# Chunked attention and a gated feed-forward layer on one core: late exp written contiguously, queries kept in mod-3 order, no block-diagonal query tile, and the first two blocks in a fixed list of steps

## The chip, the cores and the metric

The kernel runs on one core of a Trainium2 chip. The metric is the device time in microseconds. Before the change, three runs took 261.99, 262.46 and 265.42 us; the median is 262.46 us. The profile is of one more execution.

## The reference

Chunked attention with memory (B = 4, H = 8, S = 768, D = 64, chunks of 32 queries that see 16 keys to the left, 8 to the right and 8 memory keys), and then a gated feed-forward layer on the 3072 tokens.

```python
for c in range(S // 32):
    lo, hi = max(0, 32 * c - 16), min(S, 32 * c + 40)
    k_full = concat(mem_k, k[:, :, lo:hi]); v_full = concat(mem_v, v[:, :, lo:hi])
    scores = (q[:, :, 32 * c:32 * c + 32] @ k_full.T) / 8
    a = softmax(scores)
    attn[:, :, 32 * c:32 * c + 32] = a @ v_full
x = attn as [3072 tokens, 512]
out = (maximum(x @ w_gate, 0) * (x @ w_val)) @ w_out      # 512 -> 1536 -> 512
```

## The kernel before

The 3072 tokens are cut into eight **blocks** of 384 tokens (half a batch entry). The attention of a block is four **steps** of 96 queries against a band of 120 keys and 8 memory keys. A step is: the scores matmuls, exp on ScalarE, a multiplication with a 0/1 mask on VectorE, eight values matmuls (`L261`, one per head, which also give the row sums), a reciprocal and a normalising product on VectorE (`L270`), and a transposition into `xT`. The feed-forward part of a block is twelve **units** (`dff`, `L286`), each with four gate matmuls (`L293`), a relu on ScalarE (`L296`), four value matmuls (`L298`) and the product of the two on VectorE (`L300`), into `gvT`. After them come three **output tiles** (`outp`, `L306`) of twelve matmuls each (`L309`), copied to `o_sb` by ScalarE and stored.

The steps of blocks 3 to 7 stand inside the units of the block ahead (loop at `L557`): scores and exp ahead of units 4, 6, 8 and 10, the mask behind that unit's product, the values ahead of the unit two further on. The engines run their own instructions in order, as the code issues them; `mask` is issued after `dff`, so it stands behind that unit's product on VectorE. Units use four PSUM banks in turn (`bank()`, `NG`), so a gate matmul of one unit needs the relu or the product of two units earlier to be done.

Keys and queries are loaded as float32 with three consecutive tokens on a partition (`load3`), so that the token number modulo 3 becomes an axis `t`. After the cast they are turned, by TensorE in blocks 0 and 1 (called early), by DMA transposes on SyncE's queue in the others (`turn_k`, `turn_q`, `turn_dma`). `bands` copies the keys into the bands `kb`. In the late blocks `diag` (`L186`) copies the turned queries of two heads into a block-diagonal tile `qd`, so that one matmul of 192 columns over 128 rows gives the scores of two heads (`L237`). The queries there have the order (t, c), and the late exp (`L250`) puts them back in token order as it writes: every third element of a 16-bit row. The early scores (`L233`) are eight matmuls of 96 columns over 64 rows, with queries in token order, and the early exp (`L246`) writes runs.

Blocks 0 and 1 go through `pipe` (`L439`), ten rounds of one step each, with the casts, turns and weight loads of block 1 between them; values are gathered by selection matmuls (`gather_v`), with a leading one (`L347`) for the memory rows. The last four rounds hold one unit of block 0 each. Filler matmuls on zeros (`keep`) stand between the first rounds. Then come the other 20 units of blocks 0 and 1, and then their six output tiles, with the four steps of block 2 between them. The weights are loaded on GpSimd's queue: columns 0 to 255, 256 to 511, 512 to 1023 and 1024 to 1535 of both matrices and three pieces of `w_out`, all in a row; a one-element write into `kraw` after the last piece of `w_val` holds back the loads of block 2's keys and queries.

## Time and profile before

| | before |
|---|---|
| median of three runs | 262.46 us |
| the profiled execution | 262.1 us |
| its span, first to last instruction | 260.4 us |
| TensorE busy | 235.4 us, 90% |
| VectorE, ScalarE, GpSimd busy | 124.1, 128.4, 49.3 us |
| mean granted clock of TensorE | 0.985 of full speed |
| loads of a block's keys and of its queries | 768 KB each |
| loads of a 512-column piece of w_gate or w_val, of a piece of w_out | 512 KB each as stored |

A row of the timeline has the start in us, the duration in us, the engine, the line of the kernel, what is written and read with its shape, and how many instructions are merged in the row; in brackets stands how long the engine was idle ahead of it and what released it. The durations of matmuls are modelled and reach past the start of the next, so distances between starts are the better measure. PE is TensorE, DVE is VectorE, ACT is ScalarE, POOL is GpSimd, and SPq is the queue of DMAs that SyncE issues.

### The profile page before, as it was taken

How to read it: one execution, taken by the hardware profiler on the slowest of the kernel's cores; microseconds unless marked ns; L12 is line 12 of the kernel's file. 1: busy time of each engine (PE TensorE's matmuls, PEld its weight loads, DVE VectorE, ACT ScalarE, POOL GpSimd, SP SyncE). 2: the span in 40 equal slices, each digit the busy share in tenths (PEclk: the TensorE clock that was granted, in tenths of full speed). 3: DMA queues.
4: the chain of work that ended last, by engine and by line, in shares of the span. 5: the costliest groups of instructions: out<-in, count | busy, mean ns of one | idle time of the engine just before them, and what ended most of it. 6: DMA issues, size and time to landing. Idle time of an engine off the chain costs nothing.

```text
span 260.4 us, 4350 instructions
## 1 busy us (share of the span) xinstructions
PE 235.4 (90%) x1611; PEld 131.5 (50%) x1611; DVE 124.1 (48%) x257; ACT 128.4 (49%) x197; POOL 49.3 (19%) x96
## 2 busy tenths in 40 slices
PE   8895899999989698898989989898899998999993
PEld 3353565666444355544554555445564555446641
DVE  3776573444654057604673076605753276504410
ACT  2564554365357256643673457443772555333321
POOL 6499920000000500006000420006000500000000
PEclk9998899999999899999999999999999999999999
DMA  6999999849973997159941997179912801121012
GB/s 209 312 270 138 183 207 247 219 94 177 294 193 115 202 285 131 30 124 259 237 96 32 241 281 146 33 168 276 234 39 71 198 0 33 30 86 39 0 40 82
DMA packets 84381, 39.37 MB, mean 151 GB/s; under 512 B 57096, under 2 KB 81416, under 8 KB 84360
## 3 DMA queue, kind: packets, MB, share of 16 engines
q1 hardware_dynamic: 78408, 34.25, 54.2%
q0 software_dynamic: 5808, 4.72, 12.1%
q8 instruction: 12, 0.20, 0.3%
q10 hardware_dynamic: 144, 0.13, 0.1%
q14 instruction: 9, 0.07, 0.1%
HBM read 30.05 MB, written 6.29 MB: 140 GB/s over the span
## 4 chain that ended last, share of the span: by engine, by line
PE 56%; DVE 16%; issue 8%; DMA 7%; ACT 6%; SPq 3%; POOL 0%; ACTq 0%; DVEq 0%; POOLq 0%
PE PS L309 19%; PE PS L298 14%; PE PS L293 13%; DVE gvT L300 5%; DVE ex L257 5%; PE PS L261 4%; ACT g_relu L296 4%; DMA qT<-qn 3%; DVE x_big L270 3%; DMA vraw<-in_mem_v_dram 2%; PE PS L352 2%; DMA vx<-in_v_dram 2%; PE PS L237 2%; SPq L141 2%; DVE qd L188 1%
## 5 line engine op out<-in xcount | busy, mean ns | idle before, releaser
L300 DVE TENSOR_TENSOR gvT<-PS,g_relu 128x384 f16<-128x384 f32 x96 | 53.0, 556 | 96.3 <-PE PS L298 75.0
L293 PE MATMUL PS<-xT,w_gate_sb 128*128 128x384 f16 x384 | 78.7, 328 | 2.7 <-issue 2.2
L298 PE MATMUL PS<-xT,w_val_sb 128*128 128x384 f16 x384 | 79.1, 329 | 2.1 <-DVE gvT L300 1.9
L296 ACT ACTIVATE g_relu<-PS 128x384 f16<-128x384 f32 x96 | 47.8, 498 | 43.4 <-PE PS L293 22.4
L309 PE MATMUL PS<-w_out_sb,gvT 128*128 128x512 f16 x288 | 64.1, 379 | 0.0
L298 PEld LDWEIGHTS <-w_val_sb 128*128 128x128 f16 x384 | 37.8, 99 | 28.1 <-issue 3.8
L293 PEld LDWEIGHTS <-w_gate_sb 128*128 128x128 f16 x384 | 37.2, 98 | 25.9 <-issue 4.3
L250 ACT ACTIVATE ex<-PS 128x768 f16<-128x768 f32 x24 | 35.2, 1468 | 20.3 <-PE PS L237 20.2
L309 PEld LDWEIGHTS <-gvT 128*128 128x128 f16 x288 | 27.7, 98 | 31.4
L319 ACT COPY o_sb<-PS 128x512 f32<-128x512 f32 x23 | 13.5, 587 | 44.9 <-PE PS L309 43.0
L204 POOL COPY kb<-kT 128x320 f16<-128x320 f16 (+1 forms) x15 | 11.0, 830 | 130.2 <-DMA kT<-kn 130.2
L261 PE MATMUL PS<-vb,ex 128*128 128x66 f16 x256 | 13.6, 195 | 9.9 <-DVE ex L257 8.7
L270 DVE TENSOR_TENSOR x_big<-PS,rinv 96x512 f16<-96x512 f32 x32 | 22.0, 686 | 1.1
L261 PEld LDWEIGHTS <-ex 128*128 128x128 f16 x256 | 11.1, 99 | 20.4 <-ACT g_relu L296 15.6
L257 DVE TENSOR_TENSOR ex<-ex,mask_int 128x768 f16<-128x768 f16 x24 | 14.1, 586 | 7.3 <-ACT ex L246 3.9
L237 PE MATMUL PS<-qd,kb 128*128 128x192 f16 x96 | 11.8, 245 | 0.1
L188 DVE COPY qd<-qT 64x1536 f16<-64x1536 f16 x12 | 8.4, 696 | 4.8 <-DMA qT<-qn 4.8
L165 ACT CAST qn<-qraw 128x768 f16<-128x768 f32 x12 | 10.0, 836 | 0.0
L267 DVE RECIPROCAL rinv<-PS 96x8 f32<-96x8 f32 x32 | 6.4, 201 | 7.5 <-PE PS L261 5.4
L165 ACT CAST kn<-kraw 128x768 f16<-128x768 f32 x12 | 9.9, 827 | 0.0
L376 PE MATMUL PS<-zero 128*128 128x512 f16 x20 | 7.7, 519 | 1.3 <-DVE zero L378 1.3
L352 PE MATMUL PS<-v,step 128*120 128x512 f16 x27 | 8.8, 450 | 0.0
(90 smaller groups left out, 122.7 us busy)
## 6 DMA issues: line engine op xcount, KB each, us to landing
out_dram<-o_sb SPq DMA_DIRECT2D x23, 256.0 KB
vraw<-in_v_dram SPq DMA_DIRECT2D x24, 240.0 KB
kraw<-in_k_dram SPq DMA_DIRECT2D x7, 768.0 KB
qraw<-in_q_dram SPq DMA_DIRECT2D x7, 768.0 KB
w_out_sb<-in_moe_w_out_dram POOLq DMA_DIRECT2D x3, 512.0 KB, 18.1
w_gate_sb<-in_moe_w_gate_dram POOLq DMA_DIRECT2D x2, 512.0 KB, 10.4
w_val_sb<-in_moe_w_val_dram POOLq DMA_DIRECT2D x2, 512.0 KB, 12.0
kraw<-in_k_dram SPq DMA_DIRECT2D x2, 384.0 KB
```

The source lines that it names most:

```text
L165: eng(d.rearrange("p a t (x d) -> p a x t d", x=2), raw[c][:, i, 2 * a0:2 * a0 + 2 * na].rearrange("p (a x) t d -> p a x t d", x=2))
L237: pe.matmul(o[:, :, 0:QB].rearrange("p x (t c) -> p x t c", t=R3), lhsT=self.kb[:, a, j, :], rhs=qd_t[i][:, a].rearrange("p x (t c) -> p x ...
L250: act.activation(e.rearrange("p h (c t) -> p h t c", t=R3), s_ps.rearrange("p h (t c) -> p h t c", t=R3), ACT.Exp, scale=SCALE)
L257: dve.tensor_tensor(out=e, in0=e, in1=m8, op=ALU.mult)
L261: pe.matmul(PS[:, 2 + h // 4, VW * (h % 4):VW * (h % 4) + VW], lhsT=self.ex[:, h, :], rhs=self.vb[:, self.j, h, :], start=True, stop=True)
L270: dve.tensor_tensor(out=self.x.rearrange("p (b h d) -> p b h d", b=2, h=4), in0=o[:, :, :, 0:D], in1=rb, op=ALU.mult)
L293: pe.matmul(g_ps, lhsT=w_gate_sb[:, f, 128 * m:128 * m + 128], rhs=xTs[n][:, f, c0:c1], start=(f == 0), stop=(f == NFC - 1))
L296: act.activation(g_relu[:, 0:w], g_ps, ACT.Relu)
L298: pe.matmul(vl_ps, lhsT=w_val_sb[:, f, 128 * m:128 * m + 128], rhs=xTs[n][:, f, c0:c1], start=(f == 0), stop=(f == NFC - 1))
L300: dve.tensor_tensor(out=gvT[n][:, m, c0:c1], in0=vl_ps, in1=g_relu[:, 0:w], op=ALU.mult)
L309: pe.matmul(PS[:, o], lhsT=gvT[n][:, m, 128 * t:128 * t + 128], rhs=w_out_sb[:, m, :], start=(m == 0), stop=(m == NDC - 1))
L352: pe.matmul(o[0:BAND], lhsT=step3[:, c:c + BAND], rhs=v16[:, w, :, t, :], start=False, stop=(e == len(mm) - 1), skip_group_check=True)
```

## The change

What it does, part by part:

- **Late scores.** `qd` and `diag` are gone. Each late step has eight matmuls of 96 columns over 64 rows, which read the turned queries as they lie, in the order (t, c).
- **Late exp.** All exps have the early form and write runs; the queries stay in the order (t, c) through mask, values, normalisation and `xT`. The masks of the late blocks are built in that order.
- **Product.** For blocks 2 to 7 the product writes `gvT` in the order (t, j, c) and reads both its operands so, in runs of 32. An output tile then holds every third token, and its rows are stored 3 rows apart.
- **Blocks 0 and 1.** `pipe` is replaced by `ORDER`, a list of 190 tokens; each token issues one operation. It holds the eight steps and eight units (0 to 3 of each block). Scores have two pairs of banks in turn, `ex` four buffers. In steps 0, 2 and 3 the mask is added to the scores by matmuls with the identity (`pm`), in the other five VectorE multiplies. The keys' bands of block 0 are gathered by selection matmuls (`keys`); the memory rows of the values come by DMA (`vm16`) and not by a leading selection matmul. Filler matmuls stand only at the start.
- **Behind the list.** The 16 units left hold block 2's four steps (ahead of units 7, 9, 11, 13, values two units later), and all six output tiles stand at the end. The loads of block 2's keys and queries are held back by the piece of `w_gate` with columns 512 to 1023, and the last weight pieces are loaded after that; `w_out` is loaded behind block 2's bands and a first load of its values.

```diff
         def scores(self):
             i, j = self.n % 2, self.j
+            if self.pm:
+                m = neg[self.kd]
+                m4 = bass.AP(tensor=m.tensor, offset=m.offset, ap=[m.ap[0], [0, HP], [1, QB]])
+                for x in range(2):
+                    pe.matmul(PS[:, self.sb + x, 0:HP * QB].rearrange("p (a c) -> p a c", a=HP), lhsT=id16, rhs=m4,
+                              start=True, stop=True)
             for a in range(HP):
-                if self.early:
-                    for x in range(2):
-                        pe.matmul(PS[:, x, QB * a:QB * a + QB], lhsT=self.kb[D * x:D * x + D, a, j, :],
-                                  rhs=qp[D * x:D * x + D, i, a, QB * j:QB * j + QB], start=True, stop=True)
-                else:
-                    o = PS[:, a // 2, 256 * (a % 2):256 * (a % 2) + 256].rearrange("p (x c) -> p x c", x=2)
-                    pe.matmul(o[:, :, 0:QB].rearrange("p x (t c) -> p x t c", t=R3), lhsT=self.kb[:, a, j, :],
-                              rhs=qd_t[i][:, a].rearrange("p x (t c) -> p x t c", t=R3)[:, :, :, PP * j:PP * j + PP],
-                              start=True, stop=True)
+                for x in range(2):
+                    r = slice(D * x, D * x + D)
+                    o = PS[:, self.sb + x, QB * a:QB * a + QB]
+                    if self.early:
+                        pe.matmul(o, lhsT=self.kb[r, a, j, :], rhs=qp[r, i, a, QB * j:QB * j + QB],
+                                  start=not self.pm, stop=True, skip_group_check=self.pm)
+                    else:
+                        pe.matmul(o.rearrange("p (t c) -> p t c", t=R3), lhsT=self.kb[r, a, j, :],
+                                  rhs=qT_t[i][r, a, :, PP * j:PP * j + PP], start=True, stop=True)
...
-                s_ps = PS[:, 0:2].rearrange("p b (h c) -> p (b h) c", h=4)[:, :, 0:QB]
-                act.activation(e.rearrange("p h (c t) -> p h t c", t=R3),
-                               s_ps.rearrange("p h (t c) -> p h t c", t=R3), ACT.Exp, scale=SCALE)
+            act.activation(self.ex[:, :, 0:QB].rearrange("p (h b) c -> p b h c", b=2),
+                           PS[:, self.sb:self.sb + 2, 0:HP * QB].rearrange("p b (h c) -> p b h c", h=HP), ACT.Exp, scale=SCALE)
...
+        if n in EARLY:
+            dve.tensor_tensor(out=gvT[n][:, m], in0=vl_ps, in1=g_relu, op=ALU.mult)
+        else:
+            dve.tensor_tensor(out=gvT[n][:, m].rearrange("p (t j c) -> p t j c", t=R3, j=NJ),
+                              in0=vl_ps.rearrange("p (j t c) -> p t j c", t=R3, j=NJ),
+                              in1=g_relu.rearrange("p (j t c) -> p t j c", t=R3, j=NJ), op=ALU.mult)
...
+        if n in EARLY:
+            dst = out[n * MB + 128 * t:n * MB + 128 * t + 128, :]
+        else:
+            dst = bass.AP(tensor=out.tensor, offset=out[n * MB + t, 0].offset,
+                          ap=[[R3 * DM, 128], [1, DM]])
...
+    keep(20)
...
+        b3:P x6:A P4 S7 x7:A M5:D g7:A n4:D G6 fg00 P5 g6:A T4 e4:A fv00 M6:D
+        n5:D fg03 M7:D P6 fr00:A n6:D fg02 T5 fg01 fr03:A fm00:D e5:A fr02:A P7 n7:D T6 fv03 fv01 e6:A T7 fm03:D
...
+    pl(raw["k"][0:1, 0, 0, 0, 0:1], w_gate_sb[0:1, 0, 1023:1024])
     load_kq(2)
+    load_w(1024, 512)
+    cast_kx(pl, 1)
+    units = [(n, m) for m0 in (4, 8) for n in (0, 1) for m in range(m0, m0 + 4)]
+    cast3(ac, "k", 2, 0, 2)
+    cast3(ac, "k", 2, 2, 2)
+    turn_k(2)
+    cast3(ac, "q", 2, 0, 2)
+    cast3(ac, "q", 2, 2, 2)
+    turn_q(2)
+    hook = {
+        0: [lambda: load_v(2, 0), lambda: load_v(2, 1), lambda: load_v(2, 2), lambda: load_v(2, 3)],
+        1: [lambda: bands(2, pl)],
+        2: [lambda: pl(gate, vraw[0:1, 0, 1, 0, 0:1]), lambda: load_wo(0), lambda: load_wo(4), lambda: load_wo(8)],
+        6: [lambda: cast_v(dv, 2, 0, 2)],
+        7: [lambda: cast_v(dv, 2, 2, 2)],
+        12: [lambda: load_kq(3)],
+        13: [lambda: load_v(3, 0), lambda: load_v(3, 1), lambda: load_v(3, 2), lambda: load_v(3, 3)],
+    }
+    su, vu = (7, 9, 11, 13), (9, 11, 13, 15)
...
                 if u == 0:
-                    diag(n + 1)
-                if u == 1:
                     bands(n + 1, pl)
```

In the two lines of `ORDER` shown, S is a step's scores, x its exp, M its mask, P its values, n its normalisation, T and e the turn into `xT`, G and g a gather of values and its copy, fg, fr, fv and fm the four parts of a unit; the letter behind the colon is the engine.

ScalarE, from the last copies into `xT` of the early blocks to block 2. Before, the casts of block 2's keys (`kn`) and queries (`qn`) stand late among the 20 units:

```order
L280 COPY xT<-PS 128x4x96
L296 ACTIVATE g_relu<-PS 128x384 x12
L165 CAST kn<-kraw 128x4x3x64
L296 ACTIVATE g_relu<-PS 128x384
L165 CAST kn<-kraw 128x4x3x64
L296 ACTIVATE g_relu<-PS 128x384
L165 CAST qn<-qraw 128x2x2x3x64
L296 ACTIVATE g_relu<-PS 128x384
L165 CAST qn<-qraw 128x2x2x3x64
L296 ACTIVATE g_relu<-PS 128x384 x5
```

The same place now; the five relus in the second row end the list:

```order
L298 COPY xT<-PS 128x4x96
L312 ACTIVATE g_relu<-PS 128x384 x5
L177 CAST kn<-kraw 128x4x3x64 x2
L177 CAST qn<-qraw 128x2x2x3x64 x2
L312 ACTIVATE g_relu<-PS 128x384 x7
L266 ACTIVATE ex_103<-PS 128x2x4x96
```

The four casts have moved ahead of the relus of all units that are left, and stand together.

GpSimd, the weight loads. Before, all pieces stand in a row, and the two one-element writes into `kraw` and `vraw` behind them:

```order
L340 CAST v_85<-vraw 128x768 x2
L402 DMA w_gate_sb<-in_moe_w_gate_dram 128x4x512
L402 DMA w_val_sb<-in_moe_w_val_dram 128x4x512
L405 DMA w_out_sb<-in_moe_w_out_dram 128x4x512 x3
L483 MEMSET qd_97 64x4x384
L503 CAST kraw<-w_val_sb 1x1
L505 CAST vraw<-w_out_sb 32x1
```

Now, from the same piece (columns 512 to 1023) on:

```order
L444 DMA w_gate_sb<-in_moe_w_gate_dram 128x4x512
L444 DMA w_val_sb<-in_moe_w_val_dram 128x4x512
L571 CAST kraw<-w_gate_sb 1x1
L444 DMA w_gate_sb<-in_moe_w_gate_dram 128x4x512
L444 DMA w_val_sb<-in_moe_w_val_dram 128x4x512
L181 CAST kn<-kx 16x512
L213 COPY kb_99<-kT_95 128x4x3x40 x3
L585 COPY gate<-vraw 1x1
L447 DMA w_out_sb<-in_moe_w_out_dram 128x4x512 x3
```

The write that lets block 2's keys and queries load has moved ahead of the last two-matrix piece, and the loads of `w_out` behind the bands of block 2.

VectorE, the units of block 2 with the first step of block 3, before:

```order
L300 TENSOR_TENSOR gvT<-PS,g_relu 128x384
L188 COPY qd_98<-qT_96 64x4x384 x2
L300 TENSOR_TENSOR gvT<-PS,g_relu 128x384 x3
L172 CAST vb_102<-vraw 128x16x64
L257 TENSOR_TENSOR ex_103<-ex_103,mask_int 128x8x96
```

and now:

```order
L321 TENSOR_TENSOR gvT<-PS,g_relu 128x384 x4
L184 CAST vb_102<-vraw 128x16x64
L321 TENSOR_TENSOR gvT<-PS,g_relu 128x384
L273 TENSOR_TENSOR ex_103<-ex_103,mask_int 128x8x96
```

The two copies into `qd` are gone; the mask still stands behind its unit's product.

## Rows read from the trace of the kernel before

**Rows 1.** Timeline of TensorE, one late step (columns as said above).
```profile
94.23 0.81 PE L298 MATMUL PS<-xT,w_val_sb 128*128 128x384 f16 x4
94.88 0.49 PE L237 MATMUL PS<-qd,kb 128*128 128x192 f16 x4
95.21 0.81 PE L293 MATMUL PS<-xT,w_gate_sb 128*128 128x384 f16 x4
95.86 0.81 PE L298 MATMUL PS<-xT,w_val_sb 128*128 128x384 f16 x4
...
97.16 0.81 PE L298 MATMUL PS<-xT,w_val_sb 128*128 128x384 f16 x4
98.40 0.41 PE L261 MATMUL PS<-vb,ex 128*128 128x66 f16 x8 [0.43 <-DVE ex L257]
98.65 0.49 PE L237 MATMUL PS<-qd,kb 128*128 128x192 f16 x4
```
**Rows 2.** Timeline of ScalarE and VectorE in the same step.
```profile
95.15 0.56 DVE L300 TENSOR_TENSOR gvT<-PS,g_relu 128x384 f16<-128x384 f32 x1 [0.74 <-PE PS L298]
95.41 1.47 ACT L250 ACTIVATE ex<-PS 128x768 f16<-128x768 f32 x1 [0.49 <-PE PS L237]
...
96.69 0.51 ACT L296 ACTIVATE g_relu<-PS 128x384 f16<-128x384 f32 x1
97.23 0.56 DVE L300 TENSOR_TENSOR gvT<-PS,g_relu 128x384 f16<-128x384 f32 x1 [0.92 <-ACT g_relu L296]
97.70 0.55 DVE L257 TENSOR_TENSOR ex<-ex,mask_int 128x768 f16<-128x768 f16 x1
```
**Rows 3.** Groups by line: count | busy us, mean ns | idle before, releasers.
```profile
L250 ACT ACTIVATE ex<-PS 128x768 f16<-128x768 f32 x24 | 35.2, 1468 | 20.3 <-PE PS L237 20.2
L270 DVE TENSOR_TENSOR x_big<-PS,rinv 96x512 f16<-96x512 f32 x32 | 22.0, 686 | 1.1
...
L165 ACT CAST qn<-qraw 128x768 f16<-128x768 f32 x12 | 10.0, 836 | 0.0
...
L246 ACT ACTIVATE ex<-PS 128x768 f16<-128x768 f32 x8 | 6.5, 814 | 3.8 <-PE PS L233 3.8
```
**Rows 4.** Timeline of TensorE, the scores of an early step.
```profile
14.87 0.34 PE L233 MATMUL PS<-qp,kb 64*128 64x96 f16 x8
...
15.14 0.39 PE L347 MATMUL PS<-vx,selx 16*128 16x512 f16 x1
```
**Rows 5.** Waits of TensorE from 60 us on: us in total, times, longest.
```profile
PE PS L261 <- DVE ex L257: 8.7, 21, 0.4
...
PE PS L298 <- DVE gvT L300: 1.9, 3, 0.9
```
**Rows 6.** Timeline of VectorE, the copies into the block-diagonal tile.
```profile
121.02 1.55 DVE L188 COPY qd<-qT 64x1536 f16<-64x1536 f16 x2 [1.16 <-DMA qT<-qn]
```
**Rows 7.** Timeline of TensorE: first unit of block 2, and its output tiles.
```profile
88.00 0.81 PE L293 MATMUL PS<-xT,w_gate_sb 128*128 128x384 f16 x4 [2.18 <-issue]
...
109.96 7.93 PE L309 MATMUL PS<-w_out_sb,gvT 128*128 128x512 f16 x36
```
**Rows 8.** Stretches: from:to, us, busy us (count) of each engine, clock, DMA share, GB/s.
```profile
4.00:40.00 36.00, 30.47 (x294) 17.39 (x292) 23.63 (x53) 18.86 (x31) 25.36 (x42) 0.95 1.15 230
88.00:92.00 4.00, 4.00 (x16) 1.99 (x17) 0.84 (x2) 0.98 (x2) 3.13 (x8) 0.60 0.98 214
```
**Rows 9.** Timeline of TensorE, the first unit behind the last round of `pipe`.
```profile
40.25 0.81 PE L293 MATMUL PS<-xT,w_gate_sb 128*128 128x384 f16 x4 [0.57 <-ACT xT L280]
```
**Rows 10.** A contested weight piece's issue and landing; block 2's keys asked, kx used.
```profile
21.67 1.43 POOL L402 DMA_DIRECT2D w_gate_sb<-in_moe_w_gate_dram  x1
...
DMA to landing us min/median/max: 8.9/8.9/8.9
...
38.89 0.37 SPq L141 DMA_DIRECT2D kraw<-in_k_dram  x1
...
49.87 0.60 POOL L169 CAST kn<-kx 16x512 f16<-16x512 f32 x1 [8.46 <-DMA kx<-in_mem_k_dram]
```

More of the change, by code (lines that the diff above doesn't have):

```diff
@@ L64 @@
     rot = [0]
-    NG = [3]
+    NG = [2]
     def bank():
@@ L284, with turned, dff_mm, relu @@
+        def turned(self, eng):
+            eng(xTs[self.n][:, :, QB * self.j:QB * self.j + QB], self.t16)
     gvT, xTs = {}, {}
-    def dff(n, m, c0=0, c1=MB):
+    def dff_mm(n, w_sb, m):
+        o = PS[:, bank(), 0:MB]
+        for f in range(NFC):
+            pe.matmul(o, lhsT=w_sb[:, f, 128 * m:128 * m + 128], rhs=xTs[n][:, f], start=(f == 0), stop=(f == NFC - 1))
+        return o
+    def relu(g_ps):
+        g_relu = grpool.tile([128, MB], F16, name="g_relu")
+        act.activation(g_relu, g_ps, ACT.Relu)
+        return g_relu
@@ L287, in dff, with product @@
+    def product(n, m, vl_ps, g_relu):
         if n not in gvT:
             gvT[n] = gvpool.tile([128, NDC, MB], F16, name="gvT")
-        w = c1 - c0
-        g, vl = bank(), bank()
-        g_ps, vl_ps = PS[:, g, 0:w], PS[:, vl, 0:w]
-        for f in range(NFC):
-            pe.matmul(g_ps, lhsT=w_gate_sb[:, f, 128 * m:128 * m + 128], rhs=xTs[n][:, f, c0:c1],
-                      start=(f == 0), stop=(f == NFC - 1))
-        g_relu = grpool.tile([128, MB], F16, name="g_relu")
-        act.activation(g_relu[:, 0:w], g_ps, ACT.Relu)
@@ L297, in dff @@
-        for f in range(NFC):
-            pe.matmul(vl_ps, lhsT=w_val_sb[:, f, 128 * m:128 * m + 128], rhs=xTs[n][:, f, c0:c1],
-                      start=(f == 0), stop=(f == NFC - 1))
-        dve.tensor_tensor(out=gvT[n][:, m, c0:c1], in0=vl_ps, in1=g_relu[:, 0:w], op=ALU.mult)
-    def half(n, ms, c0):
-        for m in ms:
-            dff(n, m, c0, c0 + 192)
+        if n in EARLY:
[4 more added lines that the diff above has]
+                              in1=g_relu.rearrange("p (j t c) -> p t j c", t=R3, j=NJ), op=ALU.mult)
@@ L306, in outp, with dff @@
+    def dff(n, m):
+        g = relu(dff_mm(n, w_gate_sb, m))
+        product(n, m, dff_mm(n, w_val_sb, m), g)
     def outp(n, t, last=False):
@@ L382 @@
     dve.memset(selx, 0.0)
[L383 removed]
     act.activation(warm, warm, ACT.Exp)
+    steps(step3, -DPAD, -R3)
+    steps(selx, -(BAND - NMEM), -1)
     steps(id16, 0, -1)
[L386 to L389 removed]
+    for m, qb in (("first", 0), ("int", 1)):
+        build_mask(m, qb)
     for t in ex_t:
@@ L393 @@
         dve.memset(t[:, :, :, D:VW], 1.0)
-    for m, qb in (("first", 0), ("int", 1)):
-        masks[m] = build_mask(f"mask_{m}", qb)
     def load_w(c0, w, only=None):
@@ L429 @@
-    act.copy(kT_t[0][:, R3, :, 0:2 * NMEM], o)
-    bands(0, dv, (1,))
-    keep(3)
-    cast_v3(act.copy, 0, 0, 4)
-    pl(vx16, vx)
-    cast_v3(dv, 0, 4, 4)
-    masks["last"] = build_mask("mask_last", NQB - 1)
-    st = [Step(0, j) for j in range(NJ)] + [Step(1, j) for j in range(NJ)]
-    def pipe(s, mid=(), end=()):
-        if s < 2 * NJ:
-            st[s].scores()
-            st[s].soft()
-            st[s].mask()
-        for f in mid:
-            f()
-        if s < 2 * NJ:
-            gather_v(s // NJ, s % NJ)
-        if 1 <= s <= 2 * NJ:
-            st[s - 1].values()
-            st[s - 1].norm()
-        for f in end:
-            f()
-        if s >= 2:
-            st[s - 2].turn_pe(act.copy if s % 2 else dv)
@@ L485 @@
+    for m in ("first", "int", "last"):
+        product_mask(m)
     pool.memset(kn[:, 0, R3], 0.0)
@@ L532 @@
+    su, vu = (7, 9, 11, 13), (9, 11, 13, 15)
+    for u, (n, m) in enumerate(units):
+        if u == su[0]:
+            xs = att(2)
+        for j in range(NJ):
+            if u == vu[j]:
+                v_part(xs[j])
+            if u == su[j]:
+                xs[j].scores()
+                xs[j].soft()
+        dff(n, m)
+        for j in range(NJ):
+            if u == su[j]:
+                xs[j].mask()
+        for f in hook.get(u, ()):
+            f()
     outp(0, 0)
-    st = att(2)
```

364 lines of the change are left out of this document (199 added, 165 removed).

## The prediction

> **What bounds the kernel now.** I read the waits of TensorE first, then its timeline, then the engines around one step. From 40.25 us on [rows 9] TensorE is the bound: gate and value matmuls follow each other without a gap, one unit (four gate and four value matmuls of 384 columns) in 1.30 us, from 95.86 to 97.16 [rows 1]; three output tiles take 7.9 us, 2.6 each [rows 7]. The gaps left are few and have names. The largest group in the waits is the values matmul (L261) behind the masked exp: 21 waits, 8.7 us [rows 5]. Next is one hole of 2.18 us ahead of the first unit of block 2, put down to "issue": the row before shows no engine that releases it, and that unit reads the xT that four DMA transposes bring [rows 7]. Behind it the granted clock is 0.60 for the next 4 us [rows 8]. Then come three waits, 1.9 us, of value matmuls for a product on VectorE [rows 5]. Ahead of 40.25 us things are looser: from 4 to 40 us TensorE is busy 30.5 of 36 us, at a mean clock of 0.95 [rows 8].
>
> **The late exp (20 steps in blocks 3 to 7, four in block 2).** One step today: scores at 94.88; exp from 95.41, 1.47 us; the relu of the same unit can start only at 96.69; its product on VectorE starts at 97.23, the mask behind it at 97.70, and the values matmuls at 98.40 [rows 1, 2]. The value matmuls of that unit started at 95.86, the next unit's at 97.16, and those end their slot 0.65 later, at 97.81. So TensorE loses 98.40 − 97.81 = 0.59 us per step. The changed exp has the form of the early one, whose group has 8 instructions of 814 ns against 24 of 1468 ns for the late form, same elements and same function [rows 3]. With 0.65 us less the relu starts when its gate matmuls are done, and the product where an undisturbed one does, 0.92 after the first value matmul (94.23 to 95.15, [rows 1, 2]). The mask stays 0.47 behind the product and the values 0.70 behind the mask, so they come at 0.92 + 0.47 + 0.70 = 2.09 after the value matmuls, against 1.95 when nothing is waited for. A stall of 0.14 is left, 0.45 goes. The bounds are 0 (the exp stays as it is) and 0.59.
>
> Of the exp the Trainium skill, SBUF — State Buffer, section "Door 1: The DMA port swizzle", would say otherwise: it has 16-byte lines, so that 16-bit data can be strided up to 8 elements for free, and the old exp writes only every third element. By that rule the new one would gain nothing and each step would keep its 0.59. The two groups of exp in this trace, 1468 and 814 ns, do not bear the rule out.
>
> **Scores without the block-diagonal q.** Four matmuls of 192 columns become eight of 96 columns over 64 rows. The late four hold TensorE from 94.88 to 95.21, 0.33 us [rows 1]; eight of the new kind stand in the early phase, from 14.87 to the next matmul at 15.14, 0.27 us [rows 4]. That is 0.06 per step, bounds 0 and 0.06. The two copies of q into the block-diagonal tile go too; they hold VectorE 1.55 us between two products [rows 6] and are what the three waits of 1.9 us stand behind [rows 5]. I take the 1.9 as gone.
>
> **The product in permuted order.** Same elements, read and written in runs of 32. The normalisation (L270) already reads PSUM in runs of 64 with gaps and broadcasts its other operand; it takes 686 ns for 512 elements [rows 3], the product 0.56 us for 384 [rows 2], the same cost per element and start. I take no change. Even 0.1 us more would only add to the 0.14 left in each step, 24 × 0.1 = 2.4 us; nothing is cheaper than now. Output rows written 3 rows apart stay 2 KB each and lie behind other work; I take 0.
>
> **Block 2's attention moves from the output tiles into the units.** The last units of blocks 0 and 1 now cover its steps, and after the last values matmul five output tiles (13 us) lie ahead of block 2's first unit. The hole of 2.18 us is covered, and with it the 4 us at clock 0.60, which lost 4 × 0.40 = 1.6 us. If the last xT were later than those 13 us the hole would be back.
>
> **Blocks 0 and 1: the list.** Before, four units are done when the plain run of units begins at 40.25 [rows 9]; the list holds eight, so the like point before is 40.25 + 4 × 1.30 = 45.45. The list's work on TensorE is about the old one: it drops the eight leading selection matmuls and adds key matmuls and mask matmuls for three steps. If all 5.5 us of idle time from 4 to 40 and the 36 × 0.05 = 1.8 us of clock went [rows 8], the list would end at 38.1; if nothing went, at 45.45. Three engines are filled tightly in it, so I don't go below 38 and take 38.
>
> **What is late next: the four casts ahead of the units.** The four casts of block 2's keys and queries on ScalarE stood between late relus; they now stand right behind the list's last relu and ahead of the relu of the first remaining unit. ScalarE runs in order, so until block 2's queries have landed no relu passes; TensorE can do two units (four banks) and then waits. When do the queries land? They are asked for once the gate weights of columns 512 to 1023 are in. Before, that load was issued at 21.67 and landed 8.9 us later, at 30.6 [rows 10]; its place behind the same casts on GpSimd is about the same, so I keep 30.6. Then keys, kx and queries travel beside some 1.3 MB of weights (two and a half pieces). Before, the keys were issued at 38.89 beside about as much, and kx, which is issued before the queries, was there at 49.87: 11.0 us [rows 10]. Nothing shows the queries themselves. Bounds: 8.9 us (one contested weight piece) and 14.4 (kx, and 3.4 for the queries' 786,432 bytes behind it at the mean 230 GB/s of 4 to 40 us [rows 8]). I take 10, for a little less is on the way: landed at 40.7. Two casts of queries at 0.83 [rows 3] and a relu of 0.5 give 42.9 for the third unit's gate matmuls, where TensorE would have been at 38 + 2.6 = 40.6. A wait of 2.3 us, like the hole at 88.00, and I let it cost the same 1.6 us of clock: an effective 44.5.
>
> **The sum.** From 44.5: 14 units 18.2; four steps of block 2 at 0.27 + 0.25 + 0.14, 2.6 (0.25 for the values, 98.40 to 98.65 [rows 1]); six output tiles 15.6. Block 2's first unit starts at 80.9, against 88.00 + 1.6 = 89.6: 8.7 saved. Blocks 3 to 7's steps: 20 × (0.45 + 0.06) = 10.2; waits behind the q copies 1.9. Together 20.8. The profiled execution took 262.1 us (span 260.4, the rest outside it), 0.4 under the median of 262.46: 262.1 − 20.8 = 241.3, I say **241**. Alone this case reaches from 237.5 to 245.
>
> **Rivals.** (a) The queries land before the list is through with its second unit: no hold, no clock loss, 44.5 − 40.6 = 3.9 less, 237; to 233 if the list ends some us below 38. For it: nothing is queued behind the weights piece now; against it the 11.0 us of [rows 10]. 0.25. (b) The list ends at 43 to 50: it waits for evacuations in two banks, or runs partly at the low clock, since filler matmuls now stand only at its start. Then it hides the casts and sets the third unit itself, at 45.6 to 52.6: 242 to 249. 0.13. (c) The exp stays at 1.47 us, because what slows it is not the stride: 24 × 0.45 = 10.8 more, 252. Only the two groups of [rows 3] speak, and they speak clearly against it. 0.03; this is the case in which the rule of SBUF — State Buffer in the Trainium skill would hold. (d) The three w_out loads, now behind block 2's key bands and a first v load on GpSimd, are late for the first output tile. One more contested piece is 8.9 us [rows 10], so 241 + 8.9 = 250 at most. 0.06. (e) The other side: the list falls to the low clock and stays there, because its waits are spread all over it. Its matmuls, taken as the 30.5 us busy before [rows 8], would take twice that: the list would end at 38 + 30.5 = 68.5, the third unit come at 71.1: 241 − 44.5 + 71.1 = 268, slower than before. It turns where the third unit comes after 44.5 + 21 = 65.5. Against it: the old list had idle time too and kept a mean of 0.95 [rows 8]. 0.03.
>
> **Chances and range.** The forecast has 0.50. 234 to 248 leaves out the lowest of (a), the end of (b), part of (d), (c) and (e), under 0.2. Faster by over 2% (below 257.2; 2% is about what a measurement of this kernel can tell from no change): all but (e), 0.95, with 0.02 for within 2% and 0.03 for slower.
>
> **What would show it.** The late exp at 0.81 us and the values matmuls 2.09 after their unit's first value matmul; eight late scores in 0.27; no 2 us hole before block 2's units; a hole of TensorE near 40 us whose relu stands behind a ScalarE cast that waits for a load of queries, with a low clock behind it. I am wrong if the late step still loses over 0.3 us, if the list's last relu comes after 43 us, or if the first output tile waits.

## The result, and the profile after

The changed kernel takes **252.46 us** (median of four, 251.17 to 253.65), 0.961 of the kernel before, interval 0.953 to 0.969: 9.8 us less than the kernel before as it was timed beside it (262.23). The profiled execution took 251.3 us (span 249.3). On a second chip it was 254.48 us, ratio 0.973 (0.969 to 0.977). The sign is as forecast, the size is not: 20.8 us were expected, and 241 with 234 to 248 around it. Ratios leave out executions in a slower state, such as the 254.46 of e1 and the 253.95 of e9 below, so they are not quite the quotients of the medians.

The late step came out as drawn. Timeline of TensorE in the profile after, the step that answers to [rows 1] (start, us, engine, line, operation, idle time before it in brackets):

```profile
94.23 0.81 PE L307 MATMUL PS<-xT,w_val_sb 128*128 128x384 f16 x4
94.98 0.34 PE L260 MATMUL PS<-qT,kb 64*128 64x96 f16 x8
95.26 0.82 PE L307 MATMUL PS<-xT,w_gate_sb 128*128 128x384 f16 x4
95.92 0.81 PE L307 MATMUL PS<-xT,w_val_sb 128*128 128x384 f16 x4
...
97.22 0.81 PE L307 MATMUL PS<-xT,w_val_sb 128*128 128x384 f16 x4
98.01 0.41 PE L277 MATMUL PS<-vb,ex 128*128 128x66 f16 x8
98.36 0.34 PE L260 MATMUL PS<-qT,kb 64*128 64x96 f16 x8
```

ScalarE and VectorE in the same step, and the groups of the exp and of the product in blocks 2 to 7 by line (count | busy us, mean ns), for [rows 2, 3]:

```profile
95.37 0.81 ACT L266 ACTIVATE ex<-PS 128x768 f16<-128x768 f32 x1 [0.44 <-PE PS L260]
96.12 0.49 ACT L312 ACTIVATE g_relu<-PS 128x384 f16<-128x384 f32 x1
...
96.84 0.56 DVE L321 TENSOR_TENSOR gvT<-PS,g_relu 128x384 f16<-128x384 f32 x1 [0.52 <-PE PS L307]
97.31 0.55 DVE L273 TENSOR_TENSOR ex<-ex,mask_int 128x768 f16<-128x768 f16 x1
...
L266 ACT ACTIVATE ex<-PS 128x768 f16<-128x768 f32 x32 | 26.0, 811 | 16.9 <-PE PS L260 11.9 <-PE PS L257 4.1
L321 DVE TENSOR_TENSOR gvT<-PS,g_relu 128x384 f16<-128x384 f32 x72 | 40.1, 558 | 89.3 <-PE PS L307 73.8 <-ACT g_relu L312 15.1
```

The values start at 98.01, 2.09 us after the unit's value matmuls at 95.92, exactly the sum of the prediction. The slot before them ends at 97.22 + 0.65 = 97.87, so 0.14 us is lost where 0.59 was. Only the spaces ahead of the new scores are new: 94.98 instead of 94.88, and 98.36 instead of 98.01 + 0.25 = 98.26, 0.1 us each.

The front did not move: block 3's first scores start at 94.98 us, and before at 94.88 [rows 1]. From there to the end of the span it is 154.3 us (249.3 − 94.98) where it was 165.5 (260.4 − 94.88), so the whole difference of the spans, 11.1 us, lies behind that point. TensorE's timeline at the end of the list (`ORDER`, 151 tokens), at the third unit, and at block 2's first units [rows 7, 9]:

```profile
45.42 0.81 PE L307 MATMUL PS<-xT,w_gate_sb 128*128 128x384 f16 x4
...
50.81 0.81 PE L307 MATMUL PS<-xT,w_gate_sb 128*128 128x384 f16 x4 [2.63 <-ACT g_relu L312]
...
88.77 0.81 PE L307 MATMUL PS<-xT,w_gate_sb 128*128 128x384 f16 x4
...
91.64 0.81 PE L307 MATMUL PS<-xT,w_val_sb 128*128 128x384 f16 x4 [0.75 <-ACT o_sb L346]
```

The first unit behind the list starts at 45.42; the like point before, as the prediction works it out, is 45.45. The third unit is held 2.63 us by a relu. The hole of 2.18 us ahead of block 2 is gone, but its first unit still comes at 88.77 (before: 88.00), and a new wait stands right behind it: a copy into an output tile (ScalarE, 0.75 us).

Where the hold comes from is read backwards: ScalarE; then the sync queue, which asks for block 2's keys and queries; then GpSimd, which asks for the third piece of weights (columns 512 to 1023) and gates that queue.

```profile
44.23 0.49 ACT L312 ACTIVATE g_relu<-PS 128x384 f16<-128x384 f32 x1 [1.47 <-DVE gvT L319]
44.62 1.55 ACT L177 CAST kn<-kraw 128x768 f16<-128x768 f32 x2
48.81 1.56 ACT L177 CAST qn<-qraw 128x768 f16<-128x768 f32 x2 [2.63 <-DMA qraw<-in_q_dram]
...
35.64 0.37 SPq L153 DMA_DIRECT2D kraw<-in_k_dram  x1
...
28.79 1.02 POOL L223 COPY kb<-kT 128x480 f16<-128x480 f16 x1 [4.06 <-PE PS L257]
29.77 0.74 POOL L444 DMA_DIRECT2D w_gate_sb<-in_moe_w_gate_dram  x1
...
35.44 0.18 POOL L571 CAST kraw<-w_gate_sb 1x1 f32<-1x1 f16 x1 [2.40 <-DMA w_gate_sb<-in_moe_w_gate_dram]
```

A copy of key columns for block 1's last step (`b3`, L223) stands ahead of the weights' load on GpSimd and waits 4.06 us for score matmuls on TensorE. So the load goes out at 29.77, not near 21.7; the keys are asked for at 35.64, and the casts of the queries, which wait for their load, start at 48.81, 13.2 us after that. The relu at 44.23 is the list's last: the prediction had named a last relu after 43 us as a sign that it is wrong.

The list split at its first gate matmul (stretch, length, busy us of TensorE, its weight loads, VectorE, ScalarE, GpSimd, then clock, DMA share, GB/s) [rows 8]:

```profile
4.00:31.17 27.17, 23.38 (x242) 13.95 (x241) 15.63 (x35) 15.02 (x23) 16.28 (x33) 0.87 0.89 202
31.17:45.42 14.25, 12.56 (x104) 7.58 (x104) 7.04 (x15) 6.68 (x15) 4.14 (x9) 1.00 1.15 218
```

### The profile page after: what moved, and what is told of

Same layout as the page of the kernel before. It is cut to its first block, busy times and chain, and to the rows that moved or that the text cites. A ratio compares the mean times of both kernels' runs of the same rounds, so it can differ in the third digit from the quotient of the medians.

```text
span 249.3 us, 4612 instructions
## 1 busy us (share of the span) xinstructions
PE 234.6 (94%) x1742; PEld 130.4 (52%) x1742; DVE 112.8 (45%) x237; ACT 114.6 (46%) x197; POOL 47.6 (19%) x101
## 4 chain that ended last, share of the span: by engine, by line
PE 70%; DMA 12%; SPq 7%; DVE 5%; issue 2%; ACT 2%; POOL 0%; DVEq 0%; ACTq 0%
PE PS L307 40%; PE PS L332 19%; DMA qraw<-in_q_dram 5%; PE PS L277 4%; DMA vraw<-in_v_dram 3%; SPq L170 3%; PE PS L403 2%; PE PS L260 2%; DMA vraw<-in_mem_v_dram 2%; DVE x_big L286 2%; DMA xT<-x_big 2%; SPq L169 1%; DMA out_dram<-o_sb 1%; SPq L153 1%; PE PS L257 1%
## 5 line engine op out<-in xcount | busy, mean ns | idle before, releaser
L307 PE MATMUL PS<-xT,w_gate_sb 128*128 128x384 f16 x384 | 77.8, 327 | 2.8 <-ACT g_relu L312 2.6
L307 PE MATMUL PS<-xT,w_val_sb 128*128 128x384 f16 x384 | 77.5, 326 | 0.8 <-ACT o_sb L346 0.8
L312 ACT ACTIVATE g_relu<-PS 128x384 f16<-128x384 f32 x96 | 46.8, 490 | 49.1 <-DVE gvT L321 27.2
L307 PEld LDWEIGHTS <-w_gate_sb 128*128 128x128 f16 x384 | 35.3, 98 | 27.2 <-issue 3.3
L213 POOL COPY kb<-kT 128x320 f16<-128x320 f16 (+1 forms) x19 | 14.5, 852 | 117.7 <-DMA kT<-kn 117.7
L266 ACT ACTIVATE ex<-PS 128x768 f16<-128x768 f32 x32 | 26.0, 811 | 16.9 <-PE PS L260 11.9
L286 DVE TENSOR_TENSOR x_big<-PS,rinv 96x512 f16<-96x512 f32 x33 | 22.7, 687 | 1.1
L277 PEld LDWEIGHTS <-ex 128*128 128x128 f16 x264 | 10.9, 97 | 11.1 <-ACT g_relu L312 8.9
L277 PE MATMUL PS<-vb,ex 128*128 128x66 f16 x264 | 13.7, 193 | 1.6 <-DVE ex L273 0.8
L273 DVE TENSOR_TENSOR ex<-ex,mask_int 128x768 f16<-128x768 f16 x18 | 9.9, 548 | 0.0
L184 DVE CAST vb<-vraw 128x1024 f16<-128x1024 f32 x12 | 8.5, 712 | 1.6 <-DMA vraw<-in_mem_v_dram 1.5
L260 PE MATMUL PS<-qT,kb 64*128 64x96 f16 x192 | 8.3, 205 | 0.0
```

The source lines that it names most:

```text
L213: eng(dst(1, r, [[128, nj], [R3, 40]]), src(kT, TS * t + P + (r > 0), [[PP, nj], [1, 40]]))
L260: pe.matmul(o.rearrange("p (t c) -> p t c", t=R3), lhsT=self.kb[r, a, j, :], rhs=qT_t[i][r, a, :, PP * j:PP * j + PP], start=True, stop=True)
L266: act.activation(self.ex[:, :, 0:QB].rearrange("p (h b) c -> p b h c", b=2), PS[:, self.sb:self.sb + 2, 0:HP * QB].rearrange("p b (h c) -> ...
L277: pe.matmul(PS[:, 2 + h // 4, VW * (h % 4):VW * (h % 4) + VW], lhsT=self.ex[:, h, :], rhs=self.vb[:, self.j, h, :], start=True, stop=True)
L286: dve.tensor_tensor(out=self.x.rearrange("p (b h d) -> p b h d", b=2, h=4), in0=o[:, :, :, 0:D], in1=rb, op=ALU.mult)
L307: pe.matmul(o, lhsT=w_sb[:, f, 128 * m:128 * m + 128], rhs=xTs[n][:, f], start=(f == 0), stop=(f == NFC - 1))
```

## The experiments

All ratios are to the kernel before, timed on the same chip. The changed kernel itself gave 0.961 and 0.973 on two chips, so a difference of 1% between runs on different chips says nothing. Theory A: the whole gain is the late exp's. Theory B: the front is held by limits in series (the list, then block 2's loads and casts), each hiding the next. Rivals: the list is held by its low clock, or by transfers, and would give its time back if that one cause went.

**e1, the late part on the kernel before.** Eight score matmuls, the run-writing exp, mask and product in mod-3 order and the strided output rows; no block-diagonal copies; the old front and schedule.

```diff
-                    pe.matmul(o[:, :, 0:QB]..., rhs=qd_t[i][:, a]...)
+                    for x in range(2):
+                        pe.matmul(PS[:, x, QB * a:QB * a + QB]..., lhsT=self.kb[D * x:D * x + D, a, j, :],
+                                  rhs=qT_t[i][D * x:D * x + D, a, :, PP * j:PP * j + PP], ...)
...
-                act.activation(e.rearrange("p h (c t) -> p h t c", t=R3), ...)
+            act.activation(e.rearrange("p (h b) c -> p b h c", b=2), ...)
...
-                    if (n, m) == (1, 10):
-                        diag(2)
```

> The kernel before with the late part of the change alone: eight late scores of 64 rows, late exp writing runs, product in permuted order, no block-diagonal tile; blocks 0 and 1, the place of block 2's steps and all loads as before. Theory A (the late part gave all that was gained in blocks 3 to 7, the list and the moved steps nearly nothing): blocks 3 to 7 save 11.4 us as in the changed kernel, block 2's exps a little more, the hole ahead of block 2's first unit stays: 262.2 - 12 = 250 us, so within 2 us of the changed kernel's 252.5. Rival B (the list is worth a good part of the 10 us, and the late part alone less): 255 us or more.

250.93 us (249.37 to 254.46), ratio 0.958 (0.951 to 0.965): the old front with the new late part is as fast as the changed kernel. TensorE's timeline at its first unit of block 2, which still has the hole, and at block 3's first scores:

```profile
89.21 0.81 PE L283 MATMUL PS<-xT,w_gate_sb 128*128 128x384 f16 x4 [2.53 <-issue]
...
94.50 0.34 PE L232 MATMUL PS<-qT,kb 64*128 64x96 f16 x8
```

From those scores to the end of the span (249.2) it is 154.7 us, as in the changed kernel (154.3). So the list, the moved steps and the lost hole are worth nothing together that could be told from the spread.

**e2, the strided exp in the changed kernel.**

```diff
+                for x in range(2):
+                    act.activation(e.rearrange("p (h b) (c t) -> p b h t c", b=2, t=R3)[:, x],
+                                   s_.rearrange("p b (h t c) -> p b h t c", h=HP, t=R3)[:, x], ACT.Exp, scale=SCALE)
```

> The changed kernel with its late exp alone set back: it again writes with a stride of three f16 elements, and reads runs of 32, as before the change. It is issued as two halves of 384 elements a partition, one for each PSUM bank; the late mask, product and output rows are again in natural order, as the strided exp leaves them. Theory A (the run-writing exp gives the late gain): a half costs about 0.82 us (1.47 us for 768 strided elements less a fixed 0.17, halved, plus 0.17), the two 1.64 instead of 0.81, of which 0.2 us of slack swallow some; TensorE's wait before the late values rises from 0.14 us to 0.6 to 0.8 us, over 24 steps 11 to 16 us, total 263 to 269 us. Rival (the gain comes from the new score tiles, the dropped copies or the permuted product, and the exp's writing order costs nothing by itself): total 252 to 255 us, exp halves together about 1.0 us.

260.85 us, ratio 1.000 (0.997 to 1.004): without the contiguous exp nothing is left of the gain in the median. Timeline of one of its late steps, and the group of its late exp:

```profile
124.21 1.46 ACT L272 ACTIVATE ex<-PS 128x384 f16<-128x384 f32 x2 [0.43 <-PE PS L260]
...
126.07 0.81 PE L313 MATMUL PS<-xT,w_val_sb 128*128 128x384 f16 x4
127.19 0.41 PE L283 MATMUL PS<-vb,ex 128*128 128x66 f16 x8 [0.31 <-DVE ex L279]
...
L272 ACT ACTIVATE ex<-PS 128x384 f16<-128x384 f32 x48 | 35.1, 831 | 17.6 <-PE PS L260 17.6
```

The loss is smaller than the 11 to 16 us I expected: the second half starts before the first has ended, so the two take 1.46 us and not 1.64. The stall is 127.19 − 126.72 = 0.47 us, 0.33 above the 0.14; 24 × 0.33 = 7.9 us. The medians, 260.85 and 252.46, lie 8.4 apart; by the ratios, which allow for the chip, it is 1.000 against 0.961. The exp is not all of the gain, though. Behind block 3's first scores this profile takes 160.95 us (96.05 to 257.0): 6.6 more than the changed kernel's 154.3, and still 4.6 less than the 165.5 of before. Of these 4.6, 2.3 lie between the blocks, where the copies of q stood: from a block's output tiles to the next scores it is 13.06 us here and in the changed kernel, and was 13.27 to 14.00. A step is 3.70 us here, 3.77 before and 3.37 in the changed kernel. The profiled execution took 259.75 us against 262.1 before, although the medians are alike.

**e3, the third weight piece asked for ahead of `b3`.**

```diff
-... g5:A b3:P x6:A ... fr12:A wc:P fv11 ...
+... g5:A wc:P b3:P x6:A ... fr12:A fv11 ...
```

> The changed kernel with one token moved: the load of the weight columns 512 to 1023 stands ahead of the copy b3 on GpSimd, which waited 4.06 us for scores. Theory A (the casts of block 2's queries hold the units because their load is asked for late, and it is asked for late because of that wait): the load of the weight piece is issued near 25 us and not 29.8, the queries are asked for near 31 and not 37, they land before the list ends, the hole of 2.6 us goes: 249.5 us. Rival B (the transfers are bound by bandwidth, whatever the order): the queries land within 1 us of 48.8, hole and time stay, 252.5 us.

251.28 us (250.61 to 253.09), ratio 0.963 (0.956 to 0.970). The load goes out at 25.01 us and the casts of queries wait for no load; the hold is gone: the third unit comes at 47.84, 2.88 after the first (44.96) instead of 5.39. The timelines, and the waits of TensorE from 40 to 95 us (us in total, times, longest):

```profile
25.01 0.77 POOL L444 DMA_DIRECT2D w_gate_sb<-in_moe_w_gate_dram  x1
...
45.84 1.56 ACT L177 CAST qn<-qraw 128x768 f16<-128x768 f32 x2
...
47.84 0.81 PE L307 MATMUL PS<-xT,w_gate_sb 128*128 128x384 f16 x4
...
PE PS L277 <- DVE ex L273: 2.0, 2, 1.0
PE PS L307 <- ACT o_sb L346: 1.5, 1, 1.5
```

The mechanism of the hold is shown; clearing it did not give back its 2.63 us, and the total is within the spread of the changed kernel's. Two masks now stand on VectorE behind casts of block 2's values that wait for their load, and the output copies wait longer: 3.5 us in the place of 2.63 + 0.76 + 0.75.

**e4, block 1's query and value loads ahead of the memory rows on the sync queue.**

```diff
     load3(sp, "k", 1)
+    load3(sp, "q", 1)
+    load3(sp, "v", 1)
```

> The changed kernel with the loads of block 1's queries and values issued ahead of the eight small DMAs of memory rows, which wait for a cast on GpSimd and held the queue: 8 us and not 12.5 us. Theory A (the list ends at 45.4 because block 1's data come 4 us late): the cast of v behind it no longer waits 2.2 us at 21.4, the list ends 2 to 4 us earlier. Rival B (the list's TensorE is full from 19 us on and the time went into low clock and waits for evacuations before): the data come 4 us earlier and the list ends within 1 us of 45.4, total within 1 us of 252.5; if the memory rows now land later than the first values need them, later.

256.96 us, ratio 0.984 (0.977 to 0.991), slower than the changed kernel. The memory rows now land behind 1.5 MB, and the first values matmul of all waits for them:

```profile
20.34 0.41 PE L277 MATMUL PS<-vb,ex 128*128 128x66 f16 x8 [2.35 <-DMA vb<-vm]
```

The first unit behind the list comes at 47.53, and longer waits follow: 3.5 us for the relu and 2.0 for an output copy.

**e5, 22 filler matmuls between 9 and 15 us** (K5 stands for five of them).

```diff
-... q01 q01e:A q00 q00e:A cv00:P G1 S1 S0 ...
+... K5 q01 q01e:A K4 q00 q00e:A cv00:P K9 G1 S1 K4 S0 ...
```

> The changed kernel with 22 filler matmuls on zeros between 9 and 15 us of the list, where the changed kernel has TensorE idle and after it a granted clock of 0.52 from 12.5 to 19 us. Theory A (the low clock costs the list 3 us): the clock stays at 1.00 there, the list ends up to 3 us earlier; as the queries' load then holds the units, the total gains little of it, 250 to 252.5 us. Rival B (from 12.5 to 19 us the list waits for data or other engines, and TensorE's clock does not matter): the list ends at 45.4, and the total stays at 252.5 us.

252.6 us, ratio 0.968 (0.961 to 0.975). The granted clock from 12.5 to 19 us is 1.00 (0.52 in the profile after), and yet the first unit behind the list starts at 44.77, 0.65 earlier. TensorE then waits for a cast of block 1's values on GpSimd:

```profile
22.89 1.46 PE L403 MATMUL PS<-v,step 128*120 128x512 f16 x6 [0.98 <-POOL v L391]
```

The low clock is not what holds the list. A second profile of the changed kernel (a0, below) has the clock at 1.00 there without any filler, and its first unit behind the list comes at 44.24, so the low clock costs about 1.2 us of it.

**e10, no loads of block 1.** Its casts read block 0's raw tiles.

```diff
-    load3(sp, "k", 1)
...
-            load3(sp, "q", 1)
-            load3(sp, "v", 1)
...
-            raw[c][:, i, 2 * a0:...]
+            raw[c][:, 0 if n == 1 else i, 2 * a0:...]
...
```

> The changed kernel without the three loads of block 1's keys, queries and values (2.36 MB): its casts read block 0's raw tiles, so block 1 computes with block 0's rows and its part of the output is that of other data; the rest of the work, its order and the number of instructions stay. The first unit behind the list starts at 45.4 us in the changed kernel. Theory L (the list is held by the landing of data: the waits of GpSimd and VectorE for block 1's raw tiles, and the weights behind them): 2.36 MB at some 290 GB/s are 8 us of transfers; the first unit behind the list starts at 39 to 42 us and the total falls by 3 to 6 us, to 246 to 249 us. Rival D (the list is held by its chains of instructions from engine to engine, whenever the data land): 44.5 to 45.5 us, total 250.5 to 253 us, and the idle time of TensorE between 19 and 38 us stays near 3 us.

253.14 us, ratio 0.967 (0.961 to 0.972). The list is 3.4 us shorter (first unit behind it at 42.01) and the total stays. The clock in it is 1.00; set beside a0, which also had 1.00, the loads alone are 2.2 us (42.01 against 44.24). Its two parts, cut as above:

```profile
4.00:27.77 23.77, 21.27 (x243) 13.29 (x241) 15.07 (x35) 14.94 (x23) 16.86 (x33) 1.00 0.66 132
27.77:42.01 14.24, 12.56 (x104) 7.58 (x104) 7.04 (x15) 6.68 (x15) 4.19 (x9) 1.00 1.15 218
```

Only the first part gives. The second is 14.24 us with 12.56 busy, as in the profile after. The transfers in it are the same in both; in e12 below, with a DMA share of 0.91 and 196 GB/s, it is 14.25 us too, so transfers do not move it. And TensorE then waits longer at the third unit:

```profile
47.93 1.40 PE L307 MATMUL PS<-xT,w_gate_sb 128*128 128x384 f16 x4 [3.15 <-ACT g_relu L312]
```

Those four matmuls take 1.40 us: the granted clock is low behind this hold (0.83 from 47 to 57 us), as it was behind the 2.55 us of e5 (0.83 from 50 to 60), but not behind the 2.63 us of the profile after (1.00 from 50 to 60).

**e8, six output tiles instead of three** (`bufs=3` to `bufs=6` in the pool of `o_sb`).

> The changed kernel with six output tiles instead of three. Theory (TensorE's wait of 0.9 us at 91.6 us is for a copy into an output tile whose transfer has not left): that wait is gone, total 0.9 us less, 251.5 us, within the measurement's spread; rival (the copy is late for another reason, such as ScalarE's own queue): the wait stays and the total too, 252.5 us.

252.61 us, ratio 0.966 (0.960 to 0.972). The wait at 91.64 is gone, as the theory says, and in its place block 3's first scores wait 1.6 us for key columns on GpSimd, whose transposed keys are late. The old wait had covered it.

**e9, three of these together:** `wc` ahead of `b3`, six output tiles, and the casts of block 2's values two and three units later.

```diff
-        6: [lambda: cast_v(dv, 2, 0, 2)],
-        7: [lambda: cast_v(dv, 2, 2, 2)],
+        8: [lambda: cast_v(dv, 2, 0, 2)],
+        10: [lambda: cast_v(dv, 2, 2, 2)],
```

> A version meant to beat both: the changed kernel with the third weight piece asked for ahead of the copy of key columns on GpSimd's queue (which alone gave 251.3 us), six output tiles, and the two casts of block 2's values put two and three units later on VectorE, behind the masks that they held up (two waits of TensorE of 1.0 us each in that run). If the three waits simply add up: 2.0 + 1.5 us less than that run's profiled 248.4 us span, 245 us, total 247 to 248 us. Rival (each hold that goes only exposes the next, as the first three runs of the list did): span 247.5 to 248.5 us, total 250.5 to 251.5 us.

250.19 us (248.71 to 253.95), ratio 0.955 (0.947 to 0.964): close to the rival's 250.5 to 251.5. Two waits of TensorE are left behind the list:

```profile
59.86 0.42 PE L277 MATMUL PS<-vb,ex 128*128 128x66 f16 x8 [1.53 <-DVE vb L184]
...
94.39 0.34 PE L260 MATMUL PS<-qT,kb 64*128 64x96 f16 x8 [1.70 <-POOL kb L230]
```

**The changed kernel again, on the chip of the next two.**

> The changed kernel once more, on the chip on which the next two run, so that they can be set beside it: 252.5 us if it stands to the kernel before as it did (0.961 of it); a chip on which the kernel before takes 261 us would give 251 us.

254.48 us (253.08 to 256.15), ratio 0.973: more than expected here. TensorE's first unit behind the list:

```profile
44.24 0.81 PE L307 MATMUL PS<-xT,w_gate_sb 128*128 128x384 f16 x4
```

Its profile has the same hold (2.72 us) and longer waits for values (1.05) and for an output copy (2.04): the places are the same, their sizes move from run to run.

**e11, e9 with block 2's value loads ahead of the transpose of its queries,** and block 3's keys earlier.

```diff
     turn_k(2)
+    for j in range(NJ):
+        load_v(2, j)
     cast3(ac, "q", 2, 0, 2)
...
```

> The version with the third weight piece asked for early, six output tiles and later value casts (250.2 us, two waits of TensorE left in it: 1.5 us for block 2's values at 59.9 us, 1.7 us for block 3's key columns at 94.4 us), with two things more: block 2's values are asked for on the sync queue before the transpose of its queries instead of behind it, and block 3's keys and queries are loaded six units earlier, its keys cast and turned before the output products. Theory S (the places are limits in series, and each gives back its own wait only when all those behind it are cleared): both waits go, no new one over 0.8 us comes in their place, span 245 to 246 us, total 247 to 248.5 us. Rival W (the sum is bound by something else, such as the transfers): new waits of the same size show up elsewhere, total 250 to 251 us.

257.76 us, ratio 0.985 (0.981 to 0.989), 9 us and more over the 247 to 248.5 that I hoped for. The sync queue and TensorE:

```profile
48.36 0.95 SPq L169 DMA_DIRECT2D vraw<-in_v_dram  x1
...
49.41 0.81 PE L307 MATMUL PS<-xT,w_gate_sb 128*128 128x384 f16 x4 [1.18 <-ACT g_relu L312]
...
54.03 2.13 SPq L196 DMA_TRANSPOSE qT<-qn  x1
...
59.82 0.51 PE L260 MATMUL PS<-qT,kb 64*128 64x96 f16 x8 [3.75 <-DMA qT<-qn]
```

The eight loads take the queue 5.7 us to issue, the transpose goes out at 54.03 instead of 49.70 (e9), and the scores wait 3.75 us, with a mean clock of 0.73 from 60 to 70 us. The hold at the third unit is back too, with 1.18 us, though the weight piece is asked for early.

**e12, e11 without the loads of block 1.**

> The version before it in this batch without the loads of block 1's keys, queries and values, as in the earlier run without them (block 1 computes with block 0's rows). That earlier run reached the first unit behind the list 3.2 us sooner (42.0 instead of 45.4 us) and gave all of it back in the wait for block 2's queries (3.15 us). Theory S (list and queries are two limits in series, and the third weight piece is asked for in time here): the list's 3 us now stay, first unit behind the list at 42 to 43 us, no wait over 1 us at the third, total 3 us below the version with the loads, 244 to 246 us. Rival (block 2's queries come no earlier, since the third weight piece lands when it did): the wait stays at 2 to 3 us and the total within 1 us of the version with the loads.

254.47 us, ratio 0.973 (0.968 to 0.978), 3.3 us below e11, as forecast. The first unit behind the list is at 42.17 and the third at 44.83, 2.66 later, so that hold is gone with the list's 3 us kept; then the same transpose costs 6.6 us instead of 3.75. In TensorE's timeline:

```profile
44.83 0.81 PE L307 MATMUL PS<-xT,w_gate_sb 128*128 128x384 f16 x4
...
58.12 0.50 PE L260 MATMUL PS<-qT,kb 64*128 64x96 f16 x8 [6.62 <-DMA qT<-qn]
```

The third unit is 4.6 us earlier than in e11, block 2's first scores only 1.7 (59.82 there): the next limit takes back more than half, as theory B says. The total of 244 to 246 was missed by 8.5 us or more; the 6.6 us and a clock of 0.78 from 58 to 68 us behind them (2.2 us) account for that much.

**e13, e9 with block 2's steps one unit later instead,** and block 3's keys loaded two units earlier and turned ahead of the first output product.

```diff
-    su, vu = (7, 9, 11, 13), (9, 11, 13, 15)
+    su, vu = (8, 10, 12, 14), (10, 12, 14, 16)
...
-    outp(0, 0)
     cast3(ac, "k", 3, 0, 2)
-    v_part(xs[3])
     cast3(ac, "k", 3, 2, 2)
-    outp(0, 1)
     turn_k(3)
+    outp(0, 0)
+    v_part(xs[3])
+    outp(0, 1)
```

> The version with the third weight piece asked for early, six output tiles and later value casts (250.2 us median, profiled span 248.8 us, with two waits of TensorE left: 1.5 us for block 2's values, 1.7 us for block 3's key columns). Here block 2's values keep their place behind the transpose of its queries (putting them ahead held that transpose by 5.7 us and cost 3.7 to 6.6 us in the two runs before); instead block 2's four attention steps and the value casts start one unit later, which gives the values 1.3 us more, and block 3's keys are loaded two units earlier and cast and turned ahead of the first output product. Theory S (waits in series): both waits go, span 245.5 to 247 us, ratio to the kernel before 0.945 to 0.952. Rival W (something else of the same size takes their place): span 248 to 250 us, ratio 0.955 to 0.965.

**247.82 us** (247.06 to 248.44), ratio 0.945 (0.939 to 0.950): faster than the kernel before and than the changed one (0.961 and 0.973), as the theory of waits in series had it (0.945 to 0.952). From the end of the list on, TensorE waits once for over 0.4 us:

```profile
59.56 0.41 PE L277 MATMUL PS<-vb,ex 128*128 128x66 f16 x8 [1.32 <-DVE vb L184]
...
85.33 0.81 PE L307 MATMUL PS<-xT,w_gate_sb 128*128 128x384 f16 x4
```

Block 2's first unit comes at 85.33, 3.4 us before that of the changed kernel.

## Why the prediction was right or wrong

- **Late exp: right.** 811 ns forecast by the group of 814; stall 0.14 forecast and read. e1 shows that the late part is the gain, and e2 that the exp is most of it: 6.6 of the 11.2 us behind block 3's first scores. With the same elements written at a stride of three the exp takes 1.47 us (before) or 1.46 in two halves (e2), written in runs 0.81. SBUF — State Buffer in the Trainium skill, section "Door 1: The DMA port swizzle", says that 16-bit data may be strided up to 8 elements for free; for this output the rows do not agree. The stride comes together with shorter runs (32 elements for 96), and no run here parts the two.
- **Scores: right in busy time (0.28 us), wrong in what stands around them.** 0.1 us of idle time stands ahead of each group of 64-row scores, whether a unit or values come before it. A quiet block takes 26.47 us (116.16 to 142.63); twelve units are 15.6, three output tiles 7.86 and four steps of 0.66 2.64, so 0.09 is lost per step, 1.8 us over 20. The Trainium skill, TensorEngine Tiling (Array Packing), section "Key Properties", says that changing the tiling mode drains TensorE; on the way into the 64-row form the rows agree, with 0.1 us; on the way back (94.98 to 95.26) they show no more than the scores' own 0.28. The page would have named this term, which the prediction put at nothing.
- **Copies of q and product: right.** No wait of the value matmuls for a product is left, and from output tiles to the next scores 2.3 us are saved in all (forecast 1.9); the product's group is 558 ns, 556 before.
- **Hole ahead of block 2: right, and replaced.** No hole, and a clock of 1.00 from 88 to 92 us. But the work behind it was not ready either: 0.75 us for an output copy, and e8 shows 1.6 us for block 3's keys beneath that.
- **"I don't go below 38 and take 38": the step that failed first.** The list ended at 45.42. I took all idle time and clock as gone because the order is tight, and bounded it by totals of the old stretch. The work was not mis-sized, the idle time was: in a0, with the clock at 1.00 all through the list, TensorE is busy 33.4 us of the 40.2 from 4.00 to 44.24 and idle 6.9, where an end at 38 would have left 0.6. From its first gate matmul the list takes 14.24 to 14.26 us in all twelve profiles of the list, whether or not its data come early: 1.7 us of that is idle, 1.5 of it for a step's normalised values (`x_big`) on VectorE. Ahead of that point the loads of block 1 hold it in part: taking them away gave 2.2 us at equal clock (3.4 against the profile after), and the clock is worth about 1.2. What the rest of the idle time there waits for was not taken apart.
- **"I keep 30.6 ... landed at 40.7": the step that failed second.** The load was issued 8.1 us later than I put it (29.77 for 21.67) and the weights were in at 35.44 for 30.6, since I looked at its place behind casts and not at `b3`, which now stands ahead of it and waits for TensorE. From the keys' issue to the queries it was 13.2 us (13.3 to 13.7 in a0, e10 and e11), not 10; the upper bound of 14.4 was the better value. The third unit came at 50.81 instead of 42.9, though without the loss of clock. This step is the one that set the time: with the list's end alone as it was, the third unit would have come at 45.42 + 2.6 = 48.0, and in e3, with the queries early, it came at 47.84.
- **Rival (b)** had the late list and a third unit at 45.6 to 52.6, which holds the 50.81, but let the list "hide the casts". The queries came 3.4 us after the list's end (48.81 for 45.42), so it was they that set the third unit.

In sum, against block 2's first unit at 80.9: 6.3 us at the third unit (50.81 against the effective 44.5) and 1.6 behind it, of which 0.76 is a mask behind a cast. From there to block 3's first scores 0.9 more, nearly all of it the output copy (88.77 to 94.98 is 6.2 us, before 6.9 less 1.6 of clock). Behind these scores 11.2 us were saved where 12.1 were forecast: 1.8 less for the gaps ahead of the scores, and 0.9 more between the blocks and at the end. 20.8 − 7.9 − 0.9 − 0.9 = 11.1, the difference of the two spans (260.4 − 249.3).

That the front is a row of limits in series is shown by e3, e8 and e10, where one cleared limit moved the wait to the next place and left the total within 1 us or so, and by e13, where five changes together moved it from 254.48 to 247.82 us on the same chip. What the 1.7 us of idle time in the list's second part would need was not tried.

## What to carry to other kernels

An order that is meant to fill a phase is worth what the phase's successor can use: ask, for each wait that goes, which load, cast or queue is late next, and price that before taking a gain. Follow every load back to what stands ahead of it on the queue that issues it, waits on other engines too; a copy that waits 4 us for TensorE delays each load behind it by as much. In the steady part, where the exp stood in the chain ahead of TensorE's only wait, a shorter exp paid as far as that wait reached: 0.66 us less exp took the stall from 0.59 to 0.14 us a step.

## What the runs showed of the hardware that was not expected

- Two exps of 384 elements back to back, 831 ns each, take 1.46 us together: they overlap by 0.2 us (e2).
- Eight small loads (240 KB and 16 KB in turn) kept the sync queue busy for 5.7 us, 0.33 to 1.08 us each; a transpose behind them went out 4.3 us later than ahead of them (e11 against e9).
- A hold of TensorE of much the same length is followed by a low clock in some profiles (2.18 us before, 2.55 in e5, 2.70 in e2, 3.15 in e10) and not in others (2.53 us in e1, 2.63 in the profile after, 2.72 in a0).
